# Beginning the first token group of an attention-and-MLP kernel while a weight product is half summed, with two of its sums in the scores' PSUM banks and another build-time order

## The chip, the cores and the metric

One core of a Trainium2 chip. The metric is the time of one execution on the device, in microseconds (us). A profiled execution also has a span, from its first instruction to its last, some 1.8 us shorter than the time. Ratios are the mean time of one kernel's fast runs over that of the other's fast runs of the same rounds, so not quite the ratio of the medians that are quoted.

## The reference, cut to what matters

```python
def _attn_ref(q, k, v, alpha):                       # (4, 8, 768, 48) each
    for t in range(S):
        state = alpha[:, :, t, :, None] * state + np.einsum('bhd,bhe->bhde', k[:, :, t], v[:, :, t])
        y[:, :, t] = np.einsum('bhd,bhde->bhe', q[:, :, t], state)

def _moe_ref(x, w1, w2, w_out):                      # x: 3072 tokens x 384; d_ff 1024
    return np.maximum(x @ w1, x @ w2) @ w_out
```

The attention output of 3072 tokens goes through a two-branch layer.

## The kernel before

The layer is rewritten: max(a, b) = relu(a - b) + b, so out = relu(x(w1 - w2)) wo + x(w2 wo). The difference w1 - w2 is `wd`, the product w2 wo is `m16`. One scheduler, in Python, orders all instructions of all engines at build time from estimated durations; on the chip each engine runs its list in order and waits on semaphores. Names in the profile:

- `dcs`, `dtp`, `dpa`/`dpb`, `dkv`, `dy`: decay sums, transposes of q and k, scores, state update and output of two chunks (256 tokens) at a time; without the d the same for single chunks of 128. `dqt`, `dkt` are the scaled q and k, `xT` the attention output.
- `mp`: the sums of w2 wo, three column blocks of 8 matmuls; the first 4 of each need the first half of wo (`wof`), the last 4 the second half.
- `h`: x times wd, 3 matmuls for each of 8 blocks; `g` is its relu; `op`: the output, 3 matmuls from xT and m16, then 8 from g and wo. A token group is 1 to 3 chunks of which h and op are done together.

The PSUM pools, and the parts that change:

```python
    psx = ctx.enter_context(tc.tile_pool(name="psx", bufs=3, space=bass.MemoryType.PSUM))  # dcs, dtp, kv ...
    psp = ctx.enter_context(tc.tile_pool(name="psp", bufs=2, space=bass.MemoryType.PSUM))  # the scores
    psm = ctx.enter_context(tc.tile_pool(name="psm", bufs=3, space=bass.MemoryType.PSUM))  # y, mp, h, op
    # ... (cut)
    def prep_m(s, i):
        if i == 0:
            mps[s] = psm.tile([128, DM], FP32, tag="m", name="mp")
        mp = mps[s]
        for f in range(NFH * i, NFH * i + NFH):
            nc.tensor.matmul(mp, lhsT=w2T[:, f, s * 128 : (s + 1) * 128], rhs=wo16[:, f, :],
                             start=(f == 0), stop=(f == NF - 1))
    # ... (cut: the scheduler's list of operations)
    for s in range(3):
        b = Buf(rm)
        prev = None
        for i in range(2):
            prev = op("m", s, {"PE": 0.66}, lambda e, s=s, i=i: prep_m(s, i), lat=0.17,
                      deps=w2t[2 * i : 2 * i + 2] + woc[2 * i : 2 * i + 2], after=[prev] if i else [],
                      alloc=[b] if i == 0 else (), reads=[b] if i else (), prio=0.4 + 0.01 * s)
```

## Time and profile before

| | before |
|---|---|
| runs before the prediction | 146.94, 147.86, 149.18 us |
| profiled run | 146.71 us, span 144.9 us, granted clock 1.00 |
| TensorE busy | 129.7 us, 90% of the span |
| idle ahead of the second half of mp | 2.29 us |
| idle ahead of the first dtp of the second pair of chunks | 0.70 us |
| first op | 31.22 us |

The page has a row of digits for each engine, one for each fortieth of the span, in tenths. TensorE's is full from the ninth on. So what can be gained lies ahead of 31 us, or in waits that come in after it. The lines are in the prediction below.

### The profile page before, as it was taken

How to read it: one execution, taken by the hardware profiler on the slowest of the kernel's cores; microseconds unless marked ns; L12 is line 12 of the kernel's file. 1: busy time of each engine (PE TensorE's matmuls, PEld its weight loads, DVE VectorE, ACT ScalarE, POOL GpSimd, SP SyncE). 2: the span in 40 equal slices, each digit the busy share in tenths (PEclk: the TensorE clock that was granted, in tenths of full speed). 3: DMA queues.
4: the chain of work that ended last, by engine and by line, in shares of the span. 5: the costliest groups of instructions: out<-in, count | busy, mean ns of one | idle time of the engine just before them, and what ended most of it. 6: DMA issues, size and time to landing. Idle time of an engine off the chain costs nothing.

```text
span 144.9 us, 4890 instructions
## 1 busy us (share of the span) xinstructions
PE 129.7 (90%) x1969; PEld 89.4 (62%) x1969; DVE 86.6 (60%) x163; ACT 99.1 (68%) x222; POOL 83.0 (57%) x184
## 2 busy tenths in 40 slices
PE   0376884899999999999999999999999999999991
PEld 0254652677777777666666667676666676556571
DVE  4738783688496679588539866699638854300000
ACT  3544844785786797879777977686768676825831
POOL 7998300677998777675459865657576955000000
PEclk9999999999999999999999999999999999999999
DMA  4999999999989898999997999999899852010213
GB/s 120 262 341 384 387 343 235 256 231 216 176 170 269 162 215 181 237 201 185 227 237 143 251 211 214 227 197 237 171 194 239 194 145 101 8 54 7 106 54 109
DMA packets 93686, 28.62 MB, mean 197 GB/s; under 512 B 87904, under 2 KB 92128, under 8 KB 93664
## 3 DMA queue, kind: packets, MB, share of 16 engines
q1 hardware_dynamic: 93520, 28.22, 82.0%
q8 instruction: 15, 0.25, 0.7%
q10 hardware_dynamic: 144, 0.10, 0.2%
q14 instruction: 7, 0.06, 0.1%
HBM read 23.59 MB, written 4.72 MB: 195 GB/s over the span
## 4 chain that ended last, share of the span: by engine, by line
PE 73%; DMA 12%; SPq 6%; ACT 5%; issue 1%; DVE 1%; ACTq 0%
PE h L702 21%; PE op L719 19%; DMA wof<-in_moe_w_out_dram 9%; PE op L716 7%; PE y L473 6%; PE pa L414 4%; DMA w2f<-in_alpha_dram 3%; PE tp L396 3%; SPq L231 3%; PE tp L398 2%; SPq L211 2%; PE cs L338 2%; PE kv L425 1%; PE mp L691 1%; PE dtp L541 1%; PE opc L730 1%
## 5 line engine op out<-in xcount | busy, mean ns | idle before, releaser
L702 PE MATMUL h<-xT,wd 128*128 128x384 f16 (+1 forms) x216 | 36.7, 308 | 0.0
L719 PE MATMUL op<-wo,g 128*128 128x384 f16 x184 | 35.4, 326 | 0.0
L709 ACT ACTIVATE g<-h 128x384 f16<-128x384 f32 (+1 forms) x53 | 24.2, 476 | 2.9 <-PE h L702 2.2
L702 PEld LDWEIGHTS <-wd 128*128 128x128 f16 x216 | 19.5, 97 | 9.3 <-issue 0.4
L719 PEld LDWEIGHTS <-g 128*128 128x128 f16 x184 | 17.2, 98 | 11.5
L663 ACT COPY outs<-op 128x384 f32<-128x384 f32 x20 | 9.6, 478 | 14.9 <-PE op L719 14.8
L433 DVE TENSOR_TENSOR pt<-pa,u 128x512 f16<-128x512 f32 x18 | 12.4, 689 | 7.7 <-PE pb L414 6.3
L375 POOL TENSOR_TENSOR T<-w,g 48x192 f16<-48x192 f32 x30 | 15.4, 512 | 1.1
L663 ACT COPY qk<-tp 128x1024 f16<-128x1024 f16 x14 | 14.4, 1025 | 1.7 <-PE tp L398 1.7
L716 PE MATMUL op<-m,xT 128*128 128x384 f16 x69 | 15.0, 326 | 0.0
L529 POOL TENSOR_TENSOR dkt<-dkf,den 128x384 f16<-128x384 f32 x6 | 6.6, 1106 | 10.9 <-ACT den L511 10.9
L433 DVE TENSOR_TENSOR pt<-pb,u 128x512 f16<-128x512 f32 x18 | 12.2, 680 | 0.1
L444 DVE TENSOR_TENSOR w<-kv,t 48x192 f32<-48x192 f32 x24 | 8.5, 353 | 5.9 <-PE kv L425 4.6
L707 DVE TENSOR_SCALAR g<-h 128x256 f16<-128x256 f32 (+1 forms) x19 | 9.0, 482 | 3.9 <-PE h L702 3.7
L348 ACT ACTIVATE en<-cs 128x384 f32<-128x384 f32 x18 | 9.0, 498 | 2.2 <-PE cs L342 2.2
L360 POOL TENSOR_TENSOR kt<-wof,en 128x384 f16<-128x384 f32 x6 | 6.5, 1086 | 6.4 <-ACT en L348 4.9
L477 ACT CAST xT<-y 128x384 f16<-128x384 f32 x18 | 8.8, 487 | 1.9 <-PE y L473 1.4
L360 POOL TENSOR_TENSOR kt<-w2f,en 128x384 f16<-128x384 f32 x6 | 6.0, 999 | 7.0 <-issue 2.7
L360 POOL TENSOR_TENSOR kt<-w1f,en 128x384 f16<-128x384 f32 x6 | 6.0, 1000 | 5.5 <-issue 2.6
L473 PE MATMUL y<-pt,v 128*32 128x128 f16 x288 | 9.0, 220 | 0.0
L348 ACT ACTIVATE ep<-cs 128x384 f32<-128x384 f32 x18 | 9.0, 499 | 0.0
L716 PEld LDWEIGHTS <-xT 128*128 128x128 f16 x69 | 6.1, 98 | 3.1
(127 smaller groups left out, 279.4 us busy)
## 6 DMA issues: line engine op xcount, KB each, us to landing
out_dram<-outs SPq DMA_DIRECT2D x23, 192.0 KB, 3.3
w2f<-in_moe_w_dram SPq DMA_DIRECT2D x2, 768.0 KB, 7.1
wof<-in_moe_w_out_dram SPq DMA_DIRECT2D x2, 768.0 KB, 11.1
w1f<-in_moe_w_dram SPq DMA_DIRECT2D x2, 768.0 KB, 10.5
dvf<-in_v_dram SPq DMA_DIRECT2D x3, 384.0 KB, 5.7
wof<-in_alpha_dram SPq DMA_DIRECT2D x6, 192.0 KB, 3.9
wof<-in_k_dram SPq DMA_DIRECT2D x6, 192.0 KB, 4.4
wof<-in_q_dram SPq DMA_DIRECT2D x6, 192.0 KB, 4.4
```

What stands on the lines that cost most here:

```text
L348: nc.scalar.activation(out=t, in_=csv, func=ACTF.Exp, scale=scale)
L360: nc.gpsimd.tensor_mul(out=kts[n % NB][:, :, 0:D], in0=loads[n][1], in1=st[n]["en"])
L375: nc.gpsimd.tensor_mul(out=st[n]["T16"][ps, :, D * t : D * t + D], in0=st[n - 1]["w"][ps], in1=st[n]["g"][ps].unsqueeze(2).to_broadcast([D ...
L433: nc.vector.tensor_mul(out=s["pt"][:, t], in0=s["pp"][t], in1=ub)
L473: nc.tensor.matmul(y[o : o + 32, b // 4, :], lhsT=lhsT, rhs=rhs, start=start, stop=stop)
L477: nc.scalar.copy(out=xT[:, :, n * C : (n + 1) * C], in_=st[n]["y"])
L663: {"ACT": nc.scalar.copy, "DVE": nc.vector.tensor_copy, "POOL": nc.gpsimd.tensor_copy}[e](out=out, in_=in_)
L702: nc.tensor.matmul(h[:, 0:W], lhsT=wd16[:, s, f * 128 : (f + 1) * 128], rhs=xT[:, s, a : a + W], start=(s == 0), stop=(s == 2))
L707: nc.vector.tensor_relu(gts[a][:, f, 0:W], hs[a, f][:, 0:W])
L709: nc.scalar.activation(out=gts[a][:, f, 0:W], in_=hs[a, f][:, 0:W], func=ACTF.Relu)
L716: nc.tensor.matmul(op, lhsT=xT[:, s, t0 : t0 + C], rhs=m16[:, s, :], start=(s == 0), stop=False)
L719: nc.tensor.matmul(op, lhsT=gts[a][:, f, i * C : (i + 1) * C], rhs=wo16[:, f, :], start=False, stop=(f == NF - 1))
```

## The change

Its intent is to have TensorE do part of the first token group while the second half of wo is still on its way. Two of the three mp sums move to the two banks of the scores, which are free then; that leaves the banks of `psm` to h. The third sum waits whole, until wo is there. The scheduler's estimates of transfers are changed, a first group of one chunk is no longer allowed to start later groups early, and each operation's duration is multiplied by a random factor (0.85 to 1.15, seed 2) while the order is built.

```diff
+SEED, JITTER = 2, 0.3
-        self.done, self.slack = None, slack
+        self.done, self.slack, self.scale = None, slack, 1.0 + JITTER * (sched.rng.random() - 0.5)
-            cost = op.engs[e]
+            cost = op.engs[e] * op.scale
     def prep_m(s, i):
         if i == 0:
-            mps[s] = psm.tile([128, DM], FP32, tag="m", name="mp")
+            mps[s] = (psp, psp, psm)[s].tile([128, DM], FP32, tag="ppm"[s], name="mp")
-    LOAD, WLOAD = 1.06, 3.9
+    LOAD, WLOAD = 1.06, 4.1
+    LANDS = {"wo1": 2.8}
 ... (other estimates of landing times, cut)
+    MPRIO = 900
     for s in range(3):
-        b = Buf(rm)
+        b = Buf((rp, rp, rm)[s])
             prev = op("m", s, {"PE": 0.66}, ...
-                      deps=w2t[2 * i : 2 * i + 2] + woc[2 * i : 2 * i + 2], ...
-                      ..., prio=0.4 + 0.01 * s)
+                      deps=(w2t + woc if s == 2 else w2t[2 * i : 2 * i + 2] + woc[2 * i : 2 * i + 2]), ...
+                      ..., prio=(0.4 if i == 0 and s < 2 else MPRIO) + 0.01 * s)
             for o in mfirst:
-                o.after.append(g["p4", 0])
+                o.after.append(g["p3", 1])
+            mfirst[2].after.append(g["p4", 0])
-        if k == 0 or (k < WMAX // C and not idle):
+        if k == 0 or (k < WMAX // C and not idle and (a or k < 2)):
```

More of the change, by code (lines that the diff above doesn't have):

```diff
@@ L2 @@
+import random
 from contextlib import ExitStack
@@ L62, in __init__ @@
         self.refill = None
+        self.rng = random.Random(SEED)
     def start(self, op):
@@ L798 @@
         if x[0] == "d":
-            dloads_of(int(x[1]), 0.3 * int(x[1]))
+            dloads_of(int(x[1]), (0.2, 0.5, 1.2)[int(x[1])])
         else:
@@ L802 @@
             fn, to = {"w2": (load_w2, lw2), "wo": (load_wo, lwo), "w1": (load_w1, lw1)}[x[:2]]
-            prev = to[i] = op(x, i, {"SP": WLOAD / 2}, lambda e, i=i, fn=fn: fn(i), lat=1.6, after=[prev], prio=0.5)
+            prev = to[i] = op(x, i, {"SP": WLOAD / 2}, lambda e, i=i, fn=fn: fn(i), lat=LANDS.get(x, 2.0), after=[prev], prio=0.5)
     w2c = [[op("w2c", (s, i), c, lambda e, s=s, i=i: prep_w2(e, s, i), deps=[lw2[i]], prio=-0.5)
@@ L830 @@
             prev = op("m", s, {"PE": 0.66}, lambda e, s=s, i=i: prep_m(s, i), lat=0.17,
-                      deps=w2t[2 * i : 2 * i + 2] + woc[2 * i : 2 * i + 2], after=[prev] if i else [],
-                      alloc=[b] if i == 0 else (), reads=[b] if i else (), prio=0.4 + 0.01 * s)
+                      deps=(w2t + woc if s == 2 else w2t[2 * i : 2 * i + 2] + woc[2 * i : 2 * i + 2]), after=[prev] if i else [],
+                      alloc=[b] if i == 0 else (), reads=[b] if i else (), prio=(0.4 if i == 0 and s < 2 else MPRIO) + 0.01 * s)
             if i == 0:
```

## The prediction

> **What bounds the kernel now.** I read the page's busy shares first, then the 40 slices, then TensorE's waits, and last TensorE's own timeline around the places where it stops.
>
> ```profile
> PE 129.7 (90%) x1969; PEld 89.4 (62%) x1969; DVE 86.6 (60%) x163; ACT 99.1 (68%) x222; POOL 83.0 (57%) x184
> PE   0376884899999999999999999999999999999991
> PEclk9999999999999999999999999999999999999999
> ```
>
> TensorE is busy 90% of the 144.9 us span and from the ninth slice on (a slice is 3.6 us, so from about 29 us) it is full to the end; no other engine is. A full row says only that matmuls lie end to end, so I checked the pace: in the last stage 24 matmuls of 384 columns took 3.90 us in the chain, 162 ns each. They run at one pace, so TensorE's work sets the time from 29 us on. The room is in the first eight slices. TensorE's waits between 0 and 60 us give it:
>
> ```profile
> PE dcs L496 <- ACT dloga L486: 6.0, 2, 4.0
> PE mp L691 <- ACT wo L663: 2.3, 1, 2.3
> PE dpa L558 <- ACT dqk L663: 1.5, 1, 1.5
> PE dpa L558 <- DVE dqk L663: 0.8, 1, 0.8
> PE dtp L541 <- DVE dqt L527: 0.7, 1, 0.7
> ...
> PE tp L396 <- ACT qk L663: 0.2, 1, 0.2
> ```
>
> Columns: who waited for whom, us in total, how often, the longest. The first, third and fourth lie before 15.1 us, when the loads still arrive. The second and fifth are the ones that the change can touch. From 55 us on the same view lists no wait at all. Where the two stand is in the timeline of TensorE (start, length, what, and in brackets the idle time before it):
>
> ```profile
> 17.63 0.51 PE L635 MATMUL dy<-dqk,dT 112*32 112x128 f16 x12
> 18.07 1.02 PE L635 MATMUL dy<-dpt,dv 64*32 64x128 f16 x64
> 19.02 2.27 PE L691 MATMUL mp<-wo,w2T 128*128 128x384 f16 x12
> 23.58 2.11 PE L691 MATMUL mp<-wo,w2T 128*128 128x384 f16 x12 [2.29 <-ACT wo L663]
> ...
> 26.39 1.14 PE L702 MATMUL h<-xT,wd 128*128 128x256 f16 x9
> 28.23 0.40 PE L541 MATMUL dtp<-ident,dqt 128*128 128x128 f16 x4 [0.70 <-DVE dqt L527]
> ```
>
> The product of w2 and wo (mp, three column blocks of 8 matmuls) is half summed at 21.29 us; then TensorE idles 2.29 us, because the other half of wo is still on its way. The chain of work around it, in order of time:
>
> ```profile
> 9.31 13.36 DMA wof<-in_moe_w_out_dram
> 22.67 0.02 issue
> 22.69 0.84 ACT wo L663
> 23.53 0.04 issue
> 23.58 2.12 PE mp L691 x12
> ```
>
> That transfer was issued at 9.31 and landed at 22.67 us; its cast on ScalarE takes 0.84 us. Nothing that TensorE does moves this date.
>
> **What the Trainium skill says.** "TensorE: Matmul & The Clock Gate", Part 1, has the array at 1.2 GHz until about 3.4 us of sustained work have passed, then 2.4 GHz. The trace agrees in its pace: the 192-column matmuls start 0.16 us apart at 4 us and 0.08 us apart at 25.5 us. The row PEclk, 9 throughout, does not show it, so I read pace only. The idle 2.29 us did not bring the slow pace back (12 matmuls in 1.94 us after it). "TensorEngine Tiling (Array Packing)", Key Properties, says a change of tiling mode drains the engine. Here: three h matmuls from 97.86 should give way at 98.35, and the tiled y starts at 98.43; the last tiled pa starts at 99.14, ends its turn near 99.19, and op starts at 99.28: 0.08 to 0.09 us per change. "Perfetto Trace Analysis", Optimizing Tensor Performance, Matmuls, wants independent matmul groups to rotate through PSUM banks; that is what the change buys by placing two of the three mp sums in the two banks of the scores, leaving the three banks of h and op freer.
>
> **The change, part by part.** The random factors (seed 2, width 0.3) and the other guesses of transfer times act when the order is built, not on the chip. I compared the two built orders: both have the same 1969 matmuls of the same shapes, and nearly the same order of loads, so no engine gets less arithmetic. What moves:
>
> 1. Before wo's second half, TensorE now has 4 mp, dy, 4 mp, and then the first 9 h matmuls (the first token group, 256 columns); the third mp block waits as a whole. Before it had dy and 12 mp. Out go 4 x 0.162 = 0.65 us, in come 9 x 0.11 = 0.99 us (0.99 from the chain's nine at 28.85). These 9 need xT, hence dy. VectorE now has copies of w2T between the masks, 0.55 us each, so I expect dy to end near 19.7 rather than 19.0, xT near 20.9 (two casts, 1.05), and h from 21 to 22 us. That is inside the idle stretch: their cost there is nothing.
> 2. From 23.58 us up to the first op the path before is: 12 mp 1.94, two groups of dcs 0.87, 24 h 2.62, two dtp 0.89, scores with their two mode changes 0.44, sum 6.76, with 0.85 of waiting at dqt (the nine h end their turn at 27.38, dtp starts at 28.23): 7.61, and the trace has op at 31.22, which is 7.64. After: 16 mp 2.59, dcs 0.87, 15 h 1.64, dtp 0.89, scores 0.44, sum 6.43.
> 3. The wait at dqt should go. dcs now follows the first 8 mp, at 24.88 instead of 25.52. First dcs done 25.4, den 0.42, dep 0.39, dqt 1.15 gives 27.4 us; TensorE reaches dtp after 8 mp, dcs, 8 mp, 6 h at 23.58+1.30+0.87+1.29+0.65 = 27.69. So op begins near 30.0 us in place of 31.22: **1.2 us**.
> 4. From the first op on, the new order changes between tiled and plain matmuls 47 times instead of 50: 3 x 0.085 = 0.25 us. The one wait there, 0.18 us, may or may not go; I count nothing.
> 5. The last token group has 256 columns instead of 384. The work is the same in sum, and the last matmuls, eviction and stores (from 141.95 to 144.9) are of one form in both. Nothing.
>
> Sum: 1.2 + 0.25 = **1.4 us** off the span, all of it from TensorE's early idle time but the 0.25.
>
> **Rivals.**
> Gated all the same: the second half of wo lands at 22.7 in both, h lies in a hole that was free, and a new wait (dqt, or a relu that frees the bank for the fourth h) gives the gain back. For it: the margin at dtp is only 0.3 us, and ScalarE now has wo, relu, dloga, m ahead of den. Against: each of these is under 0.9 us and TensorE has work beside them. It would leave 0.3 to 0.7 us: 147.3 us.
> Slow clock: TensorE pauses more between 15 and 19 us, for the w2T copies and the later mask, so the doubling of pace may come later than the 18 to 19 us of before. In the hole that costs nothing; if the pace is still half at 23.58, 16 mp cost up to 2.6 us more, though only until the next window: 148 to 149 us. Against: TensorE had 2.29 us idle there before and kept its pace, and now idles less.
> New stalls later: the order was built with falsified durations, and a 110 us stretch that was full to 0.18 us can only lose. For it: narrower or uneven runs of h (15 in a row at 256 columns, 0.33 us per bank, against relus of 0.36 to 0.41 on ScalarE and VectorE). Against: with relus on two engines and three banks this holds. It would cost 0.5 to 2 us: 147 to 149 us.
> A large gain: idle time after 21 us is 2.29 + 0.85 + 0.18 + at most 0.25 of mode changes, 3.6 us or 2.4%, and the cast of wo cannot come earlier; more than 2% would need nearly all of it.
>
> **Range and chances.** The three times before are 146.94, 147.86 and 149.18, so a median of three is loose by some 0.7 us. 147.86 - 1.4 = 146.4 us. Adding the noise to a gain that I put between 0.3 and 2.3: 144.9 to 148.0. Over 2% faster (below 144.9) is nearly ruled out by the idle time there is: 0.06. Over 2% slower needs the clock or new stalls at their worst: 0.02. Within 2%: 0.92.
>
> **What would show it.** In the changed trace: nine h matmuls before the second half of mp, starting near 21 us; the idle time before mp cut from 2.29 to about 1.5 us; mp going on at 23.6; no or a small wait at dtp; the first op at 30.0 +- 0.4 us; TensorE full from there; and a span of about 143.5. Wrong would be: wo landing more than 0.5 us off 22.67, h at half pace, or a wait of over 0.3 us on TensorE after 32 us. If op starts at 30 and the span is still 145, the loss is in the later order and not in the start.

## The result, and the profile after

The changed kernel took 145.80 us in the median (145.48, 145.79, 145.80, 145.99), the kernel before 147.80 (146.94 to 149.18) beside it; the ratio of the fast runs is 0.9881, with an interval from 0.9835 to 0.9928. All four runs of the changed kernel had a granted clock of 1.00 and spans of 143.7 to 144.2 us. Executions over 1.5% slower than the fastest of the same kernel are left out of the means.

The page of the changed kernel, busy shares and TensorE's slices:

```profile
PE 130.5 (91%) x1969; PEld 88.5 (61%) x1969; DVE 91.6 (64%) x171; ACT 94.2 (65%) x215; POOL 82.3 (57%) x183
PE   0459975899999999999999999999999999999991
```

The same 1969 matmuls, the same full row from the ninth slice on, and a span of 144.0 in place of 144.9. TensorE's waits up to 60 us (who waited for whom, us, times, longest):

```profile
...
PE mp L697 <- ACT wo L669: 1.9, 1, 1.9
...
PE dtp L547 <- DVE dqt L533: 0.7, 1, 0.7
...
PE h L708 <- ACT xT L662: 0.4, 1, 0.4
```

The wait ahead of mp went from 2.3 to 1.9 us, a new one of 0.4 ahead of h came in, and the wait at dtp is as long as it was. TensorE's timeline there:

```profile
18.82 0.82 PE L697 MATMUL mp<-wo,w2T 128*128 128x384 f16 x4
20.04 1.14 PE L708 MATMUL h<-xT,wd 128*128 128x256 f16 x9 [0.40 <-ACT xT L662]
23.10 1.46 PE L697 MATMUL mp<-wo,w2T 128*128 128x384 f16 x8 [1.92 <-ACT wo L669]
...
26.56 0.82 PE L708 MATMUL h<-xT,wd 128*128 128x256 f16 x6
28.06 0.40 PE L547 MATMUL dtp<-ident,dqt 128*128 128x128 f16 x4 [0.68 <-DVE dqt L533]
...
30.39 0.66 PE L722 MATMUL op<-m,xT 128*128 128x384 f16 x3
```

Nine h lie in the idle stretch, as intended. At dtp TensorE is only 0.17 us ahead of the kernel before (28.06 for 28.23), but by then it has done 15 h instead of 9. Those six are 0.65 us (6 x 0.109), and with the 0.17 they make, to 0.01 us, the 0.83 us by which the first op is early (30.39 for 31.22). The loads did not land alike in the two runs: the second half of wo came at 22.20 us here and at 22.67 in the kernel before, so mp restarted 0.48 us earlier (23.10 for 23.58). From that restart to the first op the path is 7.29 us for 7.64; TensorE lost the rest of its head start in the wait at dtp. The last matmul starts 0.91 us earlier (140.76 for 141.67), so the rest, 110.37 us against 110.45, is the same.

What holds dtp is told by the chain that ended last, in order of time:

```profile
17.81 8.70 DMA dqf<-in_q_dram
...
26.61 1.41 DVE dqt L533
28.01 0.05 issue
28.06 0.62 PE dtp L547 x8
```

Before, the chain ran here through the second half of wo and the exponentials on ScalarE. Now it runs through the load of q, which lands at 26.51 us, and a dqt of 1.41 us. In the kernel before q had landed at 26.79, only 0.2 us ahead of the end of dep: a floor close beneath the wait that the change was to remove, which I had not looked for. (The length of that dqt is a second floor; see "Earlier q".)

### The profile page after: what moved, and what is told of

Same layout as the page of the kernel before. It is cut to its first block, busy times and chain, and to the rows that moved or that the text cites. A ratio compares the mean times of both kernels' runs of the same rounds, so it can differ in the third digit from the quotient of the medians.

```text
span 144.0 us, 4891 instructions
## 1 busy us (share of the span) xinstructions
PE 130.5 (91%) x1969; PEld 88.5 (61%) x1969; DVE 91.6 (64%) x171; ACT 94.2 (65%) x215; POOL 82.3 (57%) x183
## 3 DMA queue, kind: packets, MB, share of 16 engines
HBM read 23.59 MB, written 4.72 MB: 197 GB/s over the span
## 4 chain that ended last, share of the span: by engine, by line
PE 78%; SPq 11%; DMA 6%; DVE 1%; issue 1%; ACT 0%; DVEq 0%
PE h L708 21%; PE op L725 21%; PE op L722 8%; SPq L217 7%; PE y L479 6%; DMA dqf<-in_q_dram 6%; PE pa L420 4%; PE tp L402 3%; PE tp L404 3%; SPq L237 3%; PE cs L344 2%; PE kv L431 2%; PE dtp L547 2%; PE dy L641 2%; SPq L247 1%; PE cs L348 1%
## 5 line engine op out<-in xcount | busy, mean ns | idle before, releaser
L708 PE MATMUL h<-xT,wd 128*128 128x384 f16 (+1 forms) x216 | 36.0, 308 | 0.4 <-ACT xT L662 0.4
L715 ACT ACTIVATE g<-h 128x384 f16<-128x384 f32 (+1 forms) x53 | 22.9, 459 | 4.7 <-PE h L708 4.3
L669 ACT COPY qk<-tp 128x1024 f16<-128x1024 f16 x13 | 13.2, 1016 | 5.8 <-PE tp L404 5.7
L713 DVE TENSOR_SCALAR g<-h 128x384 f16<-128x384 f32 (+1 forms) x19 | 9.6, 520 | 11.5 <-PE h L708 11.3
L669 ACT COPY outs<-op 128x384 f32<-128x384 f32 x14 | 6.7, 478 | 15.6 <-PE op L725 15.6
L535 POOL TENSOR_TENSOR dkt<-dkf,den 128x384 f16<-128x384 f32 x6 | 5.9, 993 | 10.4 <-ACT den L517 10.4
L366 POOL TENSOR_TENSOR kt<-wof,en 128x384 f16<-128x384 f32 x6 | 6.0, 999 | 9.2 <-ACT en L354 7.8
L389 POOL TENSOR_TENSOR t<-w,g 128x192 f32<-128x192 f32 x12 | 6.0, 504 | 4.1 <-DVE w L448 2.4
```

Of the source, the lines that this page charges most:

```text
L366: nc.gpsimd.tensor_mul(out=kts[n % NB][:, :, 0:D], in0=loads[n][1], in1=st[n]["en"])
L669: {"ACT": nc.scalar.copy, "DVE": nc.vector.tensor_copy, "POOL": nc.gpsimd.tensor_copy}[e](out=out, in_=in_)
L708: nc.tensor.matmul(h[:, 0:W], lhsT=wd16[:, s, f * 128 : (f + 1) * 128], rhs=xT[:, s, a : a + W], start=(s == 0), stop=(s == 2))
L713: nc.vector.tensor_relu(gts[a][:, f, 0:W], hs[a, f][:, 0:W])
L715: nc.scalar.activation(out=gts[a][:, f, 0:W], in_=hs[a, f][:, 0:W], func=ACTF.Relu)
```

## The experiments

My theory ("hole" below): the gain is TensorE's order around the hole ahead of the second half of mp; the seed only picks among orders. Rivals: the early h are worth little, since dtp is held by the load of q (gate); the gain is a lucky set of transfers; the seed does it. Three sets of runs followed, on three different chips; within a set each timed kernel has six runs. Full times are read beside what each profile shows between 18 and 31 us: when TensorE restarts mp, and the first op.

### The two kernels again

No edit.

> The kernel before, unchanged, to learn how far the loads and the span wander from run to run. Theory A (the gain of the change is order alone, the loads are the same): wo lands at 22.2 to 22.7 us, the wait ahead of the second half of mp stays 2.0 to 2.4 us, the first op at 30.8 to 31.3 us, ratio to itself 1.00 +- 0.004. Rival B (the gain was a lucky run): spans of this kernel reach 144.0 as often as 145.

> The changed kernel, unchanged. Theory A: first op at 30.2 to 30.5 us, span 143.7 to 144.3, ratio 0.988 +- 0.005. Rival B: ratio 0.995 or more.

> The changed kernel a third time, as a control for the three others. It was 0.988 and 0.997 of the kernel before in two sets. Theory 'real but small' (0.8 to 1.2 us earlier at the first op, seen in both profiles): ratio 0.990 to 0.996, first op 30.2 to 30.5. Rival 'none': ratio 0.998 or more.

> The changed kernel beside them, for pairing. From the three sets so far (0.988, 0.997, 0.994): ratio 0.988 to 0.998; the profile has either the fast pace and a first op at 30.0 to 30.4, or half pace after the idle and a first op near 32.

| set | changed kernel, mean us of all runs (their number) | kernel before, the same | ratio of fast runs, interval |
|---|---|---|---|
| first | 145.76 (4) | 147.93 (4) | 0.9881 [0.9835, 0.9928] |
| after_again | 147.02 (6) | 147.06 (11) | 0.9970 [0.9917, 1.0022] |
| after_third | 146.59 (6) | 147.06 (11) | 0.9937 [0.9878, 0.9996] |
| after_fourth | 146.63 (6) | 147.33 (11) | 0.9971 [0.9929, 1.0012] |

The kernel before against itself gave 0.9951 [0.9894, 1.0007], so a set of six is good to about half a per cent. In the three later sets the fast runs average 146.53 us (16) and 147.03 us (31): 0.3%, not the 1.2% of the first set. So by the full times after_again went to rival B, and after_third and after_fourth fell within the smaller gain expected for them. The profile of before_again missed what was expected of it (a wait of 0.94 us ahead of mp, the first op at 31.53).

What makes the difference stands beside each run's time: its mean granted clock, over the whole span. It comes in steps, 1.00 (0.995 to 1), 0.988 (0.985 to 0.988), 0.977. The sets after the first give:

| in the three later sets | runs at 1.00, mean us | runs at 0.988 or less, mean us |
|---|---|---|
| changed kernel | 8 runs, 146.06 | 8 runs, 147.00 |
| kernel before | 31 runs, 147.03 | none |
| left out | before: 148.59 | changed: 148.64, 148.35; before: 149.60 |

At full clock the changed kernel is 1.0 us ahead (146.06 for 147.03, a ratio of 0.993). It loses that whenever its clock drops, which it did in 10 of 18 runs here and in none of the first four; the kernel before did in 1 of 33 beside it, and in none of six runs of an exact copy. What a step of 0.012 is will be seen in two profiles below.

The profiles of the changed kernel were all taken at full clock. Its first op stands at 30.39, 30.32, 30.00 and 30.38 us in four of them. The kernel before has 31.22, and 31.23 in the variant below that leaves its later order alone; its own second profile was slow and is not compared. So the lead at the first op is 0.95 us on average, close to the 1.0 us between the full-clock runs. But wo does not land alike in them, so the path from the restart of mp to the first op says more. It is 7.64 us in the kernel before and in that variant (restart at 23.58 and 23.59). In the changed kernel it is 7.29 in the two profiles with wo at 22.2 us, and 6.43 in the two with wo at 22.66 and 22.98. At the same restart, then, the changed order is 1.2 us ahead, as after_third shows:

```profile
23.57 1.46 PE L697 MATMUL mp<-wo,w2T 128*128 128x384 f16 x8 [1.89 <-ACT wo L669]
...
30.00 0.66 PE L722 MATMUL op<-m,xT 128*128 128x384 f16 x3
```

Where wo came earliest, the path is only 0.35 us shorter, for the reason given under "Earlier q".

### The early h put back

```diff
   mp x4, dy, mp x4,
-  h x9, mp x8, dcs, dcs, ...
+  mp x8, h x9, dcs, dcs, ...
```

> The changed kernel with one move: the nine early h matmuls (and their three relus) are put behind the eight second-half mp matmuls; every other instruction keeps its place (two dloga on ScalarE let one relu in between). Theory 'hole' (my prediction: the early h are free, so putting them back costs their time): first op 0.9 to 1.0 us later than in the changed kernel, near 31.3, span 144.9. Rival 'gate' (dqt waits for the q load, which lands near 26.5 whatever TensorE does, so h put behind only fills the wait at dtp): first op 0.1 to 0.4 us later, near 30.6, span 144.1 to 144.4; the 0.68 us wait at dtp shrinks to 0 to 0.4.

Median 148.12 us, ratio 1.0014 [0.9946, 1.0082] from its fast runs. Neither expectation came true as written: the first op of the profiled run, which was slow and of clock 0.988, stands at 33.17 us. TensorE's timeline of that run:

```profile
19.34 0.82 PE L699 MATMUL mp<-wo,w2T 128*128 128x384 f16 x4
23.81 2.49 PE L699 MATMUL mp<-wo,w2T 128*128 128x384 f16 x8 [3.65 <-ACT wo L671]
26.09 1.83 PE L710 MATMUL h<-xT,wd 128*128 128x256 f16 x9
```

The idle time is now one stretch of 3.65 us. After it the eight mp take 2.28 us from their start to that of the next operation, where the changed kernel takes 1.30, and nine h take 1.68 instead of 0.98. The stretches of time of the same run (busy time of PE, PEld, DVE, ACT and POOL, then the granted clock, the third from the last):

```profile
20.00:24.00 4.00, 0.34 (x3) 0.12 (x2) 2.87 (x3) 1.34 (x3) 0.00 (x0) 1.00 1.12 271
24.00:26.00 2.00, 2.00 (x8) 0.98 (x7) 0.00 (x0) 0.52 (x1) 0.00 (x0) 0.52 0.94 218
26.00:28.00 2.00, 2.00 (x13) 1.49 (x12) 0.46 (x2) 0.38 (x2) 0.00 (x0) 0.63 1.05 271
```

In stretches of half a microsecond the clock is 0.50 from about 24.1 to 27.5 us. Half pace for 3.4 us out of 146.8 is a mean of 1 - 0.5 x 3.4 / 146.8 = 0.988: the step. So a run's mean clock counts such stretches, 0.977 being two. Four of this kernel's six runs have 0.988 or less (147.87 to 148.65 us), the other two 146.28 and 146.87; the changed kernel's two full-clock runs beside it took 145.95 and 146.56. At full clock putting the h back thus costs 0.3 us, on two runs each, nearer to "gate" than to "hole" but too few to tell them apart. Which part of the change gives the 1.0 us at full clock is therefore not shown by full times.

### The seed alone

```diff
 (kernel before)
+SEED, JITTER = 2, 0.3
-            cost = op.engs[e]
+            cost = op.engs[e] * op.scale
```

> The kernel before with the random factors (seed 2, width 0.3) alone; sums in the old banks, old guesses of transfer times. Theory 'structure' (banks and priorities make the gain, the seed only picks among equal orders): no gain, ratio 0.995 to 1.02. Rival 'order' (the seed makes it): ratio near 0.99.

152.10 us, ratio 1.0338 [1.0285, 1.0392]: slower than either expectation, so the seed is no gain by itself. TensorE's waits after 14 us begin so:

```profile
PE dy L640 <- DVE dpt L574: 6.9, 2, 6.3
```

The perturbed order put both halves of wd ahead of the masks on VectorE. The second wd waits for w1, so the masks come at 22.56 us and dy waits 6.3 us behind them; its granted clock from 20 to 30 us is 0.51. What the seed does depends on the structure that it is drawn for. The opposite run, the new structure without the random factors, was not made, so the seed's share in the changed kernel stays open.

### Earlier q

```diff
-  load alpha, k, q, v (chunks 3 and 4, all heads)
+  load alpha, then k and q of heads 0 to 3, k and q of heads 4 to 7, then v
```

> The changed kernel with the k and q loads of the second two chunks cut in two by heads, so that the first half of q lands about 1.4 us earlier; the order on every compute engine is the same. Theory 'gate' (the q load sets when dtp may begin): where wo lands near 22.2, the wait at dtp (0.68 us) falls under 0.1 and the first op starts at 29.5 to 29.8 in place of 30.39, dkv at 31.5 in place of 32.28; where wo lands near 23.0, TensorE reaches dtp by itself at 28.0 and nothing changes at all. Rival 'ScalarE' (dep, not the load, sets dqt): dtp wait stays 0.5 or more in the first case.

Ratio 0.9963 [0.9910, 1.0015]. Four of six runs had a clock of 0.986 to 0.988 (146.65 to 147.49 us), the other two took 145.58 and 145.68; the four full-clock runs of the changed kernel beside it took 145.10 to 147.03, so no gain can be told. The profiled run is one of the slower-clocked. The first half of q landed at 25.92 us, but wo only at 23.26. TensorE's timeline, then the stretches of time:

```profile
20.81 1.16 PE L709 MATMUL h<-xT,wd 128*128 128x256 f16 x9 [0.45 <-DVE wd L674]
24.16 2.70 PE L698 MATMUL mp<-wo,w2T 128*128 128x384 f16 x8 [2.19 <-ACT wo L670]
```

```profile
24.00:26.00 2.00, 1.84 (x6) 0.86 (x6) 0.88 (x3) 1.33 (x4) 0.00 (x0) 0.55 1.08 259
26.00:28.00 2.00, 2.00 (x20) 1.60 (x19) 0.18 (x1) 0.85 (x2) 0.00 (x0) 0.59 1.25 272
```

The clock is 0.50 from about 24.2 to 27.6 us, right behind the hole, and the first op came at 32.23. Every compute engine has the order of the changed kernel here, and the changed kernel's own slower runs have the same mean clock of 0.988. In its four profiles, at full clock, the idle time was 1.89 to 2.01 us; here it was 2.19. So the changed kernel seems to stand near an edge. Whether q is the gate was not answered by this run.

It is answered, in part, by the changed kernel's own profiles. In two of them wo landed at 22.2 us and TensorE waited 0.68 us at dtp; in the two where wo landed at 22.66 and 22.98 it did not wait, and the first op came no later. Their dqt tells why. VectorE and GpSimd, first in the changed kernel's first profile:

```profile
26.61 1.40 DVE L533 TENSOR_TENSOR dqt<-dqf,dep 128x384 f16<-128x384 f32 x1 [2.10 <-DMA dqf<-in_q_dram]
```

```profile
26.59 0.99 POOL L535 TENSOR_TENSOR dkt<-dkf,den 128x384 f16<-128x384 f32 x1
```

and in after_third:

```profile
27.03 0.56 DVE L533 TENSOR_TENSOR dqt<-dqf,dep 128x384 f16<-128x384 f32 x1 [2.06 <-DMA dqf<-in_q_dram]
```

```profile
27.05 1.40 POOL L535 TENSOR_TENSOR dkt<-dkf,den 128x384 f16<-128x384 f32 x1
```

The same dqt takes 1.40 us when the same dkt began 0.02 us ahead of it, and 0.56 us when it began 0.02 us ahead of dkt, which then takes 1.40 in place of 1.0. In the second case q landed later (26.94 for 26.51) and dtp still began earlier (27.68 for 28.06). So the wait at dtp is the load of q and 0.84 us of turn-taking with GpSimd, and the second is decided by some hundredths of a microsecond. The second is enough by itself: started at 26.61, a dqt of 0.56 us would have ended at 27.17, before TensorE came free (28.06 less 0.68). "Perfetto Trace Analysis", Optimizing Scalar/DVE Operations, in the Trainium skill has GpSimd and VectorE share an SBUF read port, which fits.

### More h in the hole

```diff
-  h x9, mp x8, dcs, dcs, mp x8, h x6, dtp, h x9, dtp, scores, op x11
+  h x15, mp x8, dcs, dcs, mp x8, h x9, dtp, dtp, op x6, scores, op x5
   # the five relus of the early h on ScalarE, ahead of its cast of wo
```

> The changed kernel with 15 h matmuls instead of 9 ahead of the second half of wo, their five relus on ScalarE ahead of its cast of wo, the other 9 ahead of dtp, and the first six op matmuls ahead of the scores. Same matmuls. Theory 'hole': the wait ahead of mp falls from 1.9 to about 1.0 to 1.3 us, dkv starts 0.6 to 1.1 us earlier than in the changed kernel (31.2 to 31.6 in place of 32.2 to 32.3), span 0.5 to 1.0 us shorter, ratio about 0.985 to 0.991. Rival 'given back later': dkv earlier, but new waits of the sum between 32 and 60 us, span as the changed kernel's within 0.3.

> Both edits. If the q load is a gate and the hole another, dkv at 30.7 to 31.5 and ratio 0.980 to 0.988. If only the hole counts, as more_h alone. If the gain is given back later, as the changed kernel.

more_h: 0.9945 [0.9889, 1.0001]. With the split loads as well: 0.9925 [0.9871, 0.9980]. Both are within reach of the changed kernel of the same set (0.9937). Only one of six runs of each had the lower clock, as one would think of a shorter hole; the five others average 146.19 and 145.85 us, the changed kernel's four at full clock 145.99. In their profiles dkv begins at 32.06 and 31.94 us; the changed kernel beside them had 31.89. So at full clock nothing was gained, and the profile says why: the idle time ahead of mp fell to 1.19 us as expected, but mp restarted 1.38 and 1.39 us after wo had landed, in place of 0.91, because ScalarE has relus to do first. The split loads did their part: the first q landed at 25.21 us in place of 27.99, and the wait of 0.28 us at the first dtp of more_h was gone. In more_h a second loss came later, at 42.1 us, with the load of alpha for a single chunk behind it:

```profile
PE cs L345 <- ACT loga L340: 1.1, 1, 1.1
```

So of "hole" and "given back later" the second is nearer. The second half of wo has to be cast before mp can go on, and whatever is put into the hole on ScalarE ahead of that cast comes back as delay.

### The hole filled with matmuls that compute nothing new

```diff
 # after_warm: the third early h group, computed five times
-        for s in range(3):
+        for s in list(range(3)) * (5 if a == 0 and f == 2 else 1):
 # best_warm: the same with the fifth group three times, on top of both edits above
 # before_warm: ahead of the first half of the third mp sum
+            for f in list(range(NFH)) * 2:
+                nc.tensor.matmul(mp, lhsT=w2T[:, f, 256:384], rhs=wo16[:, f, :], start=True, stop=True)
```

before_warm overwrites the bank and then begins the sum. All results are right.

> The kernel before with 8 matmuls more (1.3 us at the fast pace) whose result is overwritten, placed ahead of the last first-half mp group, so that they lie in the 0.9 to 2.3 us idle ahead of the second half of wo. Result unchanged. Theory 'clock' (part of this kernel's loose times are executions in which the idle time drops TensorE to half pace): the slowest of the six runs comes under 147.5, ratio 0.992 to 0.998. Rival 'loads' (the spread is from when loads land): ratio 0.998 to 1.006, spread of 2 us as before.

> The changed kernel with the third early h group computed five times over (12 matmuls more, 1.3 us), inside the 1.9 to 2.2 us idle. Result unchanged. Theory 'clock': no half pace in the profile, runs within 1.2 us of each other, ratio to before 0.985 to 0.990 in place of 0.988 to 0.997. Rival 'loads': same median and spread as the changed kernel beside it.

> Both edits of the kernel that was 0.9925 (15 early h, k and q loads cut in two), and two repeats of the last early h group (6 matmuls, 0.65 us) in the idle that is left (1.2 us). Theory 'clock': six runs at 145.0 to 146.2, ratio 0.982 to 0.988. Rival 'loads': as without the repeats, 145.2 to 147.2, ratio 0.990 to 0.995.

| | six runs, us | of them at 0.988 or less | ratio, interval |
|---|---|---|---|
| before_warm | 146.52 146.64 146.91 147.47 147.65 148.31 | 0 | 1.0010 [0.9960, 1.0060] |
| after_warm | 145.44 145.49 145.58 145.67 146.22 146.54 | 0 | 0.9916 [0.9878, 0.9954] |
| after_fourth | 145.78 146.19 146.67 146.84 147.13 147.16 | 4 | 0.9971 [0.9929, 1.0012] |
| best_warm | 145.77 146.09 146.25 146.32 146.66 146.96 | 0 | 0.9951 [0.9914, 0.9989] |

Twelve matmuls more, 1.3 us of work, make the changed kernel 0.8 us faster in the mean (145.82 for 146.63). They do nothing useful but keep TensorE busy:

```profile
19.49 2.47 PE L708 MATMUL h<-xT,wd 128*128 128x256 f16 x21 [0.45 <-DVE wd L673]
23.65 0.65 PE L697 MATMUL mp<-wo,w2T 128*128 128x384 f16 x3 [1.69 <-ACT wo L669]
```

The clock says why. None of the six runs of after_warm dropped, while 10 of the 22 of the changed kernel did, four of six in this set; if nothing had changed, a split as uneven would come up about once in 33 times within the set, and once in 20 over all sets (counted over all ways to place the drops). best_warm had no drop either, but its form without fillers had one in six, so it adds little. At full clock the fillers show no gain: the changed kernel's two such runs here took 145.78 and 146.19, a mean of 145.99. So the remedy seems to remove the drops and no more. This version beats both kernels in mean and median of its set. Theory 'clock' thus did best for after_warm, though 0.9916 is above its 0.985 to 0.990; before_warm and best_warm came out as rival 'loads' had it.

The kernel before did not gain from the same remedy (1.0010), and had nothing to gain: one of its eleven runs beside it dropped. It also has runs of 148 to 149 us at full clock, of which the loads may be a part: in before_warm's profile an h at 56.7 us waits 0.53 us for xT, which the kernel before's first profile does not have.

best_warm is worse than after_warm, and its profile shows the price of too many early h. The fifth h group needs the second half of wd, which I had not seen: it waited 1.42 us for it, ScalarE's relu and then its cast of wo stood behind it, and mp restarted at 24.74 us in place of 23.65.

```profile
22.39 1.16 PE L709 MATMUL h<-xT,wd 128*128 128x256 f16 x9 [1.42 <-DVE wd L674]
24.74 1.46 PE L698 MATMUL mp<-wo,w2T 128*128 128x384 f16 x8 [1.19 <-ACT wo L670]
```

## Why the prediction was right or wrong

The time, 145.80 us for 146.4 with a range of 144.9 to 148.0: right. By its steps:

1. The nine h in the hole: right. They began at 20.04 us (21 predicted) and left 1.92 us of idle time. I had said 1.5.
2. The first op "near 30.0 us": 30.39, then 30.32, 30.00 and 30.38. The lead of 1.2 us was 0.83 in the first pair and 0.95 in the mean of the four profiles. The sum itself, 6.43 us from the restart of mp, was met exactly in the two profiles in which wo landed as late as assumed or later; with mp back at 23.57 for the forecast's 23.58, the first op came at 30.00. In the first pair the path was 7.29, 0.86 us longer than the sum, and mp was back 0.48 us early, so the first op came 0.4 us late; that is step 3.
3. "The wait at dqt should go" failed in the first pair, and it is why step 2 was too large there. I took the time at which dqt could start from ScalarE's dep alone, and its length of 1.15 us as fixed. In the first profile q landed at 26.51 and dqt took 1.41 us, so TensorE waited 0.68 us, as long as before. The wait was gone only in the profiles in which wo came later or dqt won its turn. That the gain came nevertheless was the six h done ahead of this wait.
4. Mode changes, 0.25 us: the part after the first op got shorter by 0.08. I had counted 50 and 47 changes between tiled and plain matmuls; the traces have 68 and 64, since going from y to the scores is a change as well (a matmul of y is followed after 0.15 us by the first of pa, and one of pa pairs after 0.056 by the next). Four changes less are worth some 0.35 us by that; small new stalls, 0.20 us at a dtp at 35.75 among them, took most of it.
5. The tail: right. From the start of the last matmul to the end of the span both take 3.26 us.

Of the rivals, "slow clock" was set aside because the kernel before "kept its pace" through 2.29 us. That argument failed. A drop comes, in 10 of 22 runs of the changed kernel and 1 of 33 of the kernel before, and costs the whole gain: 147.00 us for 146.06. I had put the time at 148 to 149 us, 1.6 to 2.6 above the forecast; a drop cost 0.9. The four runs of the first set had none of it, and the kernel before was slower beside them (a mean of 147.93 us) than in the later sets (147.06 to 147.33); so their ratio, 0.9881, was not met again. "Gated all the same" was right about the place, dqt. Its size, 0.3 to 0.7 us, fits the path in the two profiles with wo at 22.2 us (0.35 shorter), but not in the two with a later wo (1.21); at full clock the gain is 1.0 us, nearer to my 1.2.

Open is what in the new order brings the drops; that they lie behind the hole is seen in two profiles of neighbouring orders, not in the changed kernel's own. The kept traces hold a hint that no view prints. Thirteen of the fourteen have clock records: the first grant of full clock comes 16.1 to 21.5 us into the span, and what follows lasts a whole number of stretches of 3.41 us (6.83, 3.41, 119.47 in the two with a drop). Cut into such stretches, TensorE was busy 0.28, 1.22 and 0.91 us of 3.41 in the one just ahead of each fall to half pace (swap_back, qk_halves, seed_alone), and at least 1.44 us in every stretch after the first grant in the ten other profiles. So a drop seems to need most of the hole to fall into one stretch, and where the stretches begin differs from run to run: the first grant stands at 17.26 and 17.39 us in swap_back and qk_halves, at 17.70 to 19.15 in the changed kernel's four, and at 18.92 to 21.53 in the kernel before and its filled form. That might also be why the kernel before seldom drops. No run tested it, and none changed one feature of the start alone.

## What to carry to other kernels

Before counting a removed wait as gain, look for the next thing to arrive at the same place: here the load of q landed 0.2 us ahead of the operation that was waited for, and with a multiplication on GpSimd beside dqt it took the wait over. Work that fills a hole on one engine is only free if what it needs on the others does not stand ahead of the thing that ends the hole. And an idle stretch of about 2 us on TensorE can cost more than its length in some runs and not in others: read each run's mean clock beside its time before explaining a spread, and try a few useless matmuls in the hole.

## What the Trainium skill lacked or had wrong

- "TensorE: Matmul & The Clock Gate" gives as a rule no idle gaps on TensorE over about 3.4 us. Here an idle time of 2.19 us, with 1.0 us of h and 0.45 us of idle ahead of it, was followed by half pace for about 3.4 us; 3.65 us was too, while 1.89 to 2.01 us in four profiles and 2.29 us in the kernel before were not. The changed kernel, one and the same program, dropped in 10 of its 22 runs. The page does say that the start of a kernel varies from run to run, with windows that run on regardless of the kernel; the gap rule needs the same warning.
- The same page advises not to trust single events of the clock, and to check a total of throttled time against a model of its cost. A run's mean granted clock served for it here: each stretch at half pace is 0.5 x 3.4 us of the span, 0.012 (0.988 for one, 0.977 for two).
- It also says that trace events of this gate can be unreliable. Here they agreed with the pace of the matmuls wherever there were any; what misled was their absence. In the kernel before the first clock record is at 18.92 us, and the views show 1.00 ahead of it, while matmuls of 192 columns started 0.16 us apart in place of 0.08; after_warm's profile has no clock record at all.
- "TensorEngine Tiling (Array Packing)" says that changing the tiling mode drains the engine, without a size. Here a change costs 0.08 to 0.10 us, also between two tiled forms (0.15 in place of 0.056 us from y to pa).
